# Attention and two MoE layers on one core: gates moved into ScalarE's copies of transposes, scalings over three engines, later weight decoding

## The chip, the cores and the metric

One core of one Trainium2 chip runs the whole program. Its engines work side by side, each through its own list of instructions in order: TensorE (PE; its weight loads are PEld), VectorE (DVE), ScalarE (ACT), GpSimd (POOL) and SyncE (SP, which issues DMAs). An instruction starts when the one ahead of it has gone and the semaphores that it waits for have come. The metric is the device time of the program in microseconds; less is better.

## The reference

Float32 throughout. `q`, `k`, `v` are (4, 8, 576, 64): batches, heads, positions, columns.

```
a     = softmax(causal(q k^T / 8));   local = a v
mem   = (phi(q) M_prev) / (phi(q) z_prev + 1e-6);   phi(x) = max(x,0) + exp(min(x,0))
g     = sigmoid(beta)                        # one number per head
x     = g * mem + (1 - g) * local            # then 2304 tokens x 512
h     = x w_in;   x = (h - tanh(h)) w_out    # MoE layer 1, 512 -> 2048 -> 512
h     = x w_in2;  out = (P(h) / Q(h)) w_out2 # MoE layer 2, rational gate
```

The MoE weights arrive as float64 words and are turned into float32 on the chip.

## The kernel before, in words

**Attention.** Two heads make a pair; there are 16 pairs (4 batches x 4). Queries come in four row blocks of 128 (`i` = 0 to 3) and one of 64 rows for both heads together (`i` = 4). For each block `scores` multiplies on PE, `least` (DVE) copies the masked scores out of PSUM and takes the row's extreme, `expo` (ACT) takes exp and the row's sum, `recip` (DVE) inverts the sum, `scale` multiplies the probabilities `p` by 1/sum and by (1 - g) (POOL, nine times per pair), `turn` (PE) transposes them into a PSUM tile `tp`, `turned` (ACT) copies that to the SBUF tile `pT`, and `values` (PE) multiplies by v. The memory part runs beside it: `phi1` to `phi3`, `norm1` to `norm3` (1/norm times g is multiplied into phi), `phiT` (PE transposes), `phiC` (ACT's copy to SBUF), `memory` (PE). Both parts add up in the PSUM tiles `pv` and `pw`; `leave` (DVE) copies these to `x`. A pair's last copies are `x<-pv` (512 columns) and `x<-pw` (64).

**Weights.** Each MoE layer has 16 chunks `f`, each with two pieces `s` (w_in, w_out). A piece is decoded by `w_decode`: ACT Abs (L575), then four DVE steps (L577, L578, L582, L585). `w_split` makes a high part (ACT, L595) and a low part (POOL, L597). `w_keep` writes the decoded piece to DRAM, and `w_back` fetches it later and splits it (ACT L618, DVE L621). `Background.tick` moves every piece in work on by one step and may start one more.

**MoE layer 1.** An item is one chunk on one tile of tokens. Four chunks (0 to 3) run on 9 tiles of 256 tokens (36 small items), the other 12 on 6 tiles of 384 (72 items). Each item has 12 matmuls in its head (`h`, L1049), the gate (ACT tanh L1078, DVE L1079, ACT high part `gh` L1084, DVE low part `gl` L1085), and 12 matmuls in its tail (`y`, L1096). The tokens' own split `xs` (L1040 ACT, L1041 POOL) is made once per tile. Layer 2 has 96 items of 384 tokens.

**What sets the order.** The attention stage is laid out by a table: event `name` of pair `n` has the time 100 n + `AT[name]`, or `OVER[n][name]` in place of it, and the events are written into the engines' lists in that order. `FILL` places small MoE heads (`h`), token splits (`xs`) and background steps (`bg`) in every period of 100, the steps only from `BG_FROM` on, and only some of them may start a new piece after `MIX_FROM`. The heads' gates and tails follow at fixed offsets. What is left of the 36 small items when the table ends is run by `advance` in a loop, one item and one `tick` per turn. Then come the 72 items with further ticks, then layer 2.

Of the kernel before, what the change touches and what calls it, by code (L numbers as in the profile page):

```python
# [19 lines left out]
P = 128  # L20
# [9 lines left out]
BG_FROM = 411.57  # L30
N_PT = 6
AGE_A, AGE_B, AGE_C = 1, 3, 4

AT = {'s1': 48.5,
 's2': -9.21,
 's3': 21.3,
 's4': 70.44,
 'm0': 4.97,
 'm1': 62.46,
 'm2': 5.74,  # L40
 'm3': 33.51,
 'm4': 78.23,
 'x00': 30.93,
 'x01': 24.67,
 'x10': 102.19,
 'x11': 85.19,
 'x20': 18.5,
 'x21': 19.67,
 'x30': 58.64,
 'x31': 69.14,  # L50
 'x40': 109.89,
 'r0': 37.01,
 'r1': 108.02,
 'r2': 41.21,
 'r3': 76.67,
 'r4': 118.34,
 'c00': 74.77,
 'c01': 56.83,
 'c10': 122.27,
 'c11': 119.0,  # L60
 'c20': 56.26,
 'c21': 59.04,
 'c30': 108.12,
 'c31': 89.73,
 'c40': 130.65,
 't0': 80.11,
 't1': 78.69,
 't2': 125.39,
 't3': 124.44,
 't4': 141.98,  # L70
 't5': 169.93,
 't6': 143.99,
 'k0': 102.22,
 'k1': 88.5,
 'k2': 137.01,
 'k3': 127.14,
 'k4': 158.58,
 'k5': 173.99,
 'k6': 164.4,
 'v0': 154.99,  # L80
 'v1': 165.34,
 'v2': 165.15,
 'v3': 157.91,
 'v4': 214.1,
 'mpv': 135.18,
 'mpw': 207.69,
 'opv': 193.7,
 'opw': 216.87,
 'f0': 96.55,
 'f1': 107.92,  # L90
 'g0': 111.95,
 'g1': 119.11,
 'phi1': -43.41,
 'phi2': -30.03,
 'phi3': -19.86,
 'norm1': 0.16,
 'norm2': 31.56,
 'norm3': 32.06,
 'load_k': 31.4,
 'load_q': -0.43,  # L100
 'load_n': 22.21,
 'load_v': 69.9}
OVER = {0: {'s1': -246.08,
     's2': -489.04,
     's3': -438.03,
     's4': -268.61,
     'm0': -364.53,
     'm1': -58.91,
     'm2': -376.8,
     'm3': -354.5,  # L110
     'm4': -107.2,
     'x00': -253.7,
     'x01': -333.4,
# [204 lines left out]
     'x10': 53.22,
     'x11': 53.59,
     'x20': 19.69,  # L320
     'x21': 35.75,
     'x30': 38.43,
     'x31': 65.04,
     'x40': 88.75,
     'r0': 40.06,
     'r1': 63.48,
     'r2': 52.17,
     'r3': 69.87,
     'r4': 94.42,
     'c00': 49.51,  # L330
     'c01': 71.71,
     'c10': 122.1,
     'c20': 58.79,
     'c30': 101.38,
     'c31': 107.83,
     'c40': 106.11,
     't0': 77.35,
     't1': 84.46,
     't2': 111.03,
     't3': 124.81,  # L340
     't4': 129.29,
     't5': 169.94,
     't6': 175.76,
     'k0': 79.21,
     'k1': 86.74,
     'k2': 118.15,
     'k3': 137.94,
     'k4': 146.79,
     'k5': 174.32,
     'k6': 181.98,  # L350
     'v0': 151.75,
     'v1': 164.52,
     'v2': 161.24,
     'v3': 147.01,
     'v4': 206.58,
     'mpv': 119.31,
     'mpw': 202.36,
     'opv': 179.54,
     'opw': 233.46,
     'f0': 100.8,  # L360
     'f1': 111.34,
     'g0': 105.32,
     'g1': 167.75,
     'phi1': -49.32,
     'phi2': -26.17,
     'phi3': -17.57,
     'norm1': -9.26,
     'norm2': 14.37,
     'norm3': 23.54,
     'load_k': 6.62,  # L370
     'load_q': 11.44,
     'load_n': 20.81,
     'load_v': 100.48},
 4: {'s1': 35.05,
     's2': -12.86,
     's3': -4.6,
     's4': 71.3,
     'm0': 1.53,
     'm1': 55.25,
     'm2': 12.98,  # L380
     'm3': 36.56,
     'm4': 82.1,
     'x00': 43.45,
     'x01': 2.11,
     'x10': 76.35,
     'x11': 85.28,
     'x21': 17.28,
     'x30': 60.58,
     'x31': 70.56,
     'x40': 103.3,  # L390
     'r0': 57.92,
     'r1': 88.17,
     'r2': 33.4,
     'r4': 122.54,
     'c00': 68.21,
     'c01': 59.63,
     'c10': 102.54,
     'c11': 117.17,
     'c20': 45.05,
     'c21': 56.72,  # L400
     'c30': 107.47,
     'c31': 91.4,
     'c40': 131.13,
     't0': 89.95,
     't2': 128.1,
     't3': 129.22,
     't4': 121.75,
     't5': 166.87,
# [41 lines left out]
KEEP = 5  # L450
# [1114 lines left out]
```

## Time and profile before

| | us |
|---|---|
| median of 3 runs | 1038.77 (1038.48 to 1040.22) |
| the profiled execution | 1039.35 |
| its span, first to last instruction | 1037.6 |
| PE busy | 1010.9 (97%) |
| DVE, ACT, POOL busy | 784.7, 701.5, 362.6 |

PE's busy time is modelled and is not PE at its peak, so the table alone doesn't say where time can be had. The stages of the span can be told by PE's lines: attention to 252.84 us (with small items in between), the rest of the small items to 328.41 us, the 72 items to about 633 us, layer 2 to the end.

### The profile page before, as it was taken

What the parts mean: (1) busy time and instruction counts of PE and PEld (TensorE: products, weight loads), DVE (VectorE), ACT (ScalarE), POOL (GpSimd) and SP (SyncE); (2) the same over time, 40 slices, a digit from 0 to 9 for tenths busy, and PEclk for the clock granted to TensorE, in tenths of its full rate; (3) what the DMA queues carried; (4) which work ended last, traced back from release to release, by engine and by line L of the source; (5) the groups of instructions that cost most, each with busy time, mean ns of one, the idle gap of its engine ahead of it and who ended that gap; (6) DMA issues with size and microseconds to landing.
All of it is one profiled execution on the core that took longest, in us unless ns stands there. A gap on an engine that the chain in (4) does not pass through costs nothing.

```text
span 1037.6 us, 18004 instructions
## 1 busy us (share of the span) xinstructions
PE 1010.9 (97%) x6446; PEld 912.2 (88%) x6446; DVE 784.7 (76%) x1759; ACT 701.5 (68%) x1492; POOL 362.6 (35%) x380
## 2 busy tenths in 40 slices
PE   7999999999988999999999999999999999999998
PEld 4766777888988999999999999999999999999997
DVE  5889999874878366757676767987877877877885
ACT  5878877785555443333333556998888888888886
POOL 4878896673543010101000101332332423323221
PEclk9999999999999999999999999999999999999999
DMA  4445556432232124444444441000000000000000
GB/s 131 124 148 146 166 133 203 140 109 73 82 103 82 41 92 122 122 128 128 136 126 123 141 144 41 21 1 32 1 11 22 1 31 1 1 31 1 22 10 31
DMA packets 37674, 82.97 MB, mean 80 GB/s; under 512 B 8528, under 2 KB 11088, under 8 KB 37584
## 3 DMA queue, kind: packets, MB, share of 16 engines
q1 hardware_dynamic: 37120, 81.55, 26.1%
q8 instruction: 51, 0.84, 0.3%
q14 instruction: 39, 0.32, 0.1%
q10 hardware_dynamic: 464, 0.27, 0.1%
HBM read 66.07 MB, written 15.73 MB: 79 GB/s over the span
## 4 chain that ended last, share of the span: by engine, by line
PE 80%; DVE 12%; ACT 4%; issue 2%; POOL 1%; DMA 0%; SPq 0%; DVEq 0%; ACTq 0%; POOLq 0%
PE h L1049 35%; PE y L1179 19%; PE y L1096 17%; PE s L857 3%; DVE p L873 3%; PE tp L925 2%; PE pv L974 2%; DVE wf L585 2%; DVE wf L582 1%; ACT p L886 1%; DVE gl L1085 1%; DVE wf L577 1%; DVE phi L789 1%; PE pw L974 1%; DVE wf L578 1%
## 5 line engine op out<-in xcount | busy, mean ns | idle before, releaser
L1049 PE MATMUL h<-xs,w 128*128 128x384 f32 (+1 forms) x2448 | 437.4, 327 | 1.6 <-POOL xs L1041 0.7
L1049 PEld LDWEIGHTS h<-xs,w 128*128 128x128 f32 x2448 | 408.2, 188 | 12.5 <-POOL xs L1041 1.3
L1096 PE MATMUL y<-gh,w 128*128 128x384 f32 (+1 forms) x864 | 216.3, 318 | 3.0 <-ACT gh L1084 2.9
L1179 PE MATMUL y<-w,gh 128*128 128x512 f32 x576 | 179.6, 393 | 0.0
L1096 PEld LDWEIGHTS y<-gh,w 128*128 128x128 f32 x864 | 152.2, 189 | 4.3 <-ACT gh L1084 3.1
L1096 PE MATMUL y<-gl,w 128*128 128x384 f32 (+1 forms) x432 | 137.6, 318 | 4.0 <-DVE gl L1085 3.9
L1041 POOL TENSOR_TENSOR xs<-x,xs 128x256 fp32r<-128x256 f32 (+1 forms) x56 | 51.3, 940 | 256.1 <-ACT xs L1040 232.8
L1078 ACT ACTIVATE g<-h 128x384 f32<-128x384 f32 (+1 forms) x108 | 49.2, 455 | 134.6 <-PE h L1049 121.0
L1079 DVE TENSOR_TENSOR g<-h,g 128x384 f32<-128x384 f32 (+1 forms) x108 | 55.2, 512 | 97.2 <-ACT g L1078 97.0
L906 POOL TENSOR_SCALAR p<-p,sm,omg 128x256 f32<-128x256 f32 (+4 forms) x143 | 109.2, 773 | 48.8 <-DVE sm L898 34.7
L1179 PEld LDWEIGHTS y<-w,gh 128*128 128x128 f32 x576 | 106.8, 188 | 17.4
L1179 PE MATMUL y<-w,gl 128*128 128x512 f32 x288 | 114.0, 396 | 0.2
L1168 POOL TENSOR_TENSOR gl<-g,gh 128x384 fp32r<-128x384 f32 x48 | 49.5, 1031 | 149.8 <-ACT gh L1166 149.8
L1168 POOL TENSOR_TENSOR gl<-vG,gh 128x384 fp32r<-128x384 f32 x47 | 50.3, 1070 | 131.2 <-ACT gh L1166 129.0
L886 ACT ACTIVATE p<-p,sm 128x128 f32<-128x128 f32 (+4 forms) x144 | 84.9, 592 | 12.2 <-DVE sm L873 8.3
L1084 ACT CAST gh<-g 128x384 fp32r<-128x384 f32 (+1 forms) x108 | 51.6, 478 | 61.2 <-PE y L1096 58.6
L1096 PEld LDWEIGHTS y<-gl,w 128*128 128x128 f32 x432 | 81.6, 189 | 5.2 <-DVE gl L1085 5.2
L1155 DVE TENSOR_TENSOR vA<-vA,vC 128x384 f32<-128x384 f32 x96 | 53.5, 558 | 42.9 <-ACT vC L1149 42.9
L873 DVE CUSTOM_DVE_ANT_0 p<-s,mask 128x512 f32<-128x512 f32 (+4 forms) x160 | 69.5, 478 | 17.3 <-PE s L857 15.2
L1085 DVE TENSOR_TENSOR gl<-g,gh 128x384 fp32r<-128x384 f32 (+1 forms) x108 | 61.8, 573 | 23.6 <-ACT gh L1084 23.6
L857 PE MATMUL s<-rk,rq 64*128 64x512 f32 (+5 forms) x320 | 71.9, 475 | 7.8 <-DVE sm L873 5.1
L1144 DVE SCALAR_TENSOR_TENSOR vA<-vA,vC 128x384 f32<-128x384 f32 x96 | 59.3, 618 | 25.2 <-ACT vC L1143 20.1
(95 smaller groups left out, 1607.2 us busy)
## 6 DMA issues: line engine op xcount, KB each, us to landing
wraw<-in_w_in_dram SPq DMA_DIRECT2D x32, 512.0 KB, 4.1
wraw<-in_w_out_dram SPq DMA_DIRECT2D x32, 512.0 KB, 4.0
wk<-wf SPq DMA_DIRECT2D x42, 256.0 KB, 4.4
wx<-wk SPq DMA_DIRECT2D x21, 512.0 KB, 3.3
qn<-in_qn_dram SPq DMA_DIRECT2D x16, 320.0 KB, 3.7
vn<-in_vn_dram SPq DMA_DIRECT2D x16, 320.0 KB, 4.3
out_dram<-o SPq DMA_DIRECT2D x18, 256.0 KB, 2.0
rk<-in_kd_dram SPq DMA_DIRECT2D x30, 144.0 KB, 2.8
```

Of the source, the lines that this page charges most:

```text
L857: nc.tensor.matmul(bank[:, c0:c0 + k1 - k0], d["rq"][r, q0:q0 + P], d["rk"][r, k0:k1], start=True, stop=True, skip_group_check=True,)
L873: nc.vector.tensor_tensor_reduce(out=v["p"][-1][:, k0:k1], in0=bank[:, c0:c0 + k1 - k0], in1=mask, scale=-0.125, scalar=3.0e38, op0=ALU.ad ...
L886: nc.scalar.activation(pt, pt, AF.Exp, bias=sm[:, 4 + e:5 + e], scale=-1.0, accum_out=sm[:, 2 * e:2 * e + 1],)
L906: eng.tensor_scalar(pt, pt, v["sm"][:, 6 + e:7 + e], og[:, c:c + 1], ALU.mult, ALU.mult)
L1049: nc.tensor.matmul(ps[:, 0:T], wi_of(layer, f, wp, k), xs[k][:, xp], start=(n == 0), stop=(n == 3 * NK - 1),)
L1079: nc.vector.tensor_tensor(v["g"], v["h"], v["g"], ALU.subtract)
L1085: self.lo.tensor_tensor(v["gl"], v["g"], v["gh"].bitcast(F32), ALU.subtract)
L1096: nc.tensor.matmul(ps, wo_of(1, f, w)[:, m * P:(m + 1) * P], v[g], start=(first and j == 0 and m % n == 0), stop=(last and j == 2), skip_g ...
L1144: nc.vector.scalar_tensor_tensor(A, A, QEPS, C, ALU.add, ALU.mult)
L1155: nc.vector.tensor_tensor(n["A"], n["A"], n["C"], ALU.mult)
L1168: eng.tensor_tensor(o["gl"], o["G"], o["gh"].bitcast(F32), ALU.subtract)
L1179: nc.tensor.matmul(acc_of[t][m], g[:, c], wo_of(2, f, w), start=(first and j == 0), stop=(last and j == 2),)
```

## The change

- `g` no longer goes into `norm2`. `phiC`'s ACT copy multiplies by it, with a column of scalars (`g4`) as its scale.
- For the row blocks 0, 2 and 3 (`LATE`), (1 - g) no longer goes into `scale`; it becomes the scale of ACT's copy in `turned`. Blocks 1 and 4 keep both factors in `scale`.
- The nine scalings of a pair are spread by `SCALES`: two on ACT (128x128 and 128x512), one on DVE (128x384), six on POOL.
- The last block's two extremes are put together with a reduce into another column.
- The low parts of layer 1's chunks that are decoded after attention go to DVE in place of POOL; those decoded in attention stay on POOL.
- `KEEP` falls from 5 to 1: one chunk, not five, is decoded in attention, written to DRAM and fetched back; eleven, not seven, are decoded directly after attention.
- A new table: background steps start later, six places per period in place of four, and the small heads start later. The program has 4 small heads and 1 tail ahead of the last matmul of attention, where it had 13 and 13.
- In the stage of 72 items steps come by a list (`TICKS_1`), and pieces of layer 2 start at least three ticks apart (`EVERY`).
- `banks`, `inside` and `N_P` are set so that nothing else changes: `PSUM_DECODE` is False, `N_P` is 1, `MIX` is True.

```diff
-BG_FROM = 411.57
+BG_FROM = 1157.58
+SCALES = "APPPPVAPP"
+LATE = (0, 2, 3)
+LOW_ATT, LOW_POST, LOW_X = "P", "V", "P"
 AT = {
- 's1': 48.5,
+ 's1': 85.61,
...
 FILL = {
- 'h': [-68.87, -232.13],
+ 'h': [-1954.49, 128.27],
- 'bg': [(-191.13, 0, 1), (187.94, 1, 1), (73.53, 0, 0), (51.79, 0, 0)],
+ 'bg': [(248.62, 1, 1), (198.68, 1, 1), (6.75, 1, 0), (59.81, 1, 0), (22.12, 1, 0),
+        (36.08, 1, 0)],
...
-KEEP = 5
+KEEP = 1
...
@@ Background.tick
+                and (self.q[self.ns][2][0] == 1 or self.now >= self.last + EVERY)
...
@@ norm2
             nc.vector.reciprocal(nrm, nrm)
-            gg = self.cp["g"][:, h:h + 2].unsqueeze(1)
-            nc.vector.tensor_tensor(nrm, nrm, gg.to_broadcast([P, NQ + 1, 2]), ALU.mult)
@@ phiC
-            nc.scalar.copy(d["phiT"][:, j0:j0 + w], d.pop(("php", k))[:, 0:w])
+            nc.scalar.activation(
+                d["phiT"][:, j0:j0 + w], d.pop(("php", k))[:, 0:w], AF.Copy,
+                scale=self.cp["g4"][:, n % NP:n % NP + 1],
+            )
@@ scale
-            eng = nc.vector if (n, i, e) == (0, NQ - 1, 0) else nc.gpsimd
-            eng.tensor_scalar(
-                pt, pt, v["sm"][:, 6 + e:7 + e], og[:, c:c + 1], ALU.mult, ALU.mult
-            )
+            how = "V" if (n, i, e) == (0, NQ - 1, 0) else SCALES[2 * i + e]
+            eng = nc.vector if how == "V" else nc.gpsimd
...
+            elif how == "A":
+                nc.scalar.activation(pt, pt, AF.Copy, scale=r)
+            else:
+                eng.tensor_scalar(pt, pt, r, None, ALU.mult)
@@ turned
-            nc.scalar.copy(t[:, 0:w, :].rearrange("r t c -> r (t c)"), ps[:, 0:w * P])
+            if i in LATE:
+                c = 2 * (n % NP) + e
+                nc.scalar.activation(
+                    dst, ps[:, 0:w * P], AF.Copy, scale=self.cp["omg"][:, c:c + 1]
+                )
+            else:
+                nc.scalar.copy(dst, ps[:, 0:w * P])
@@ after attention
-            bg.add(1, f, w_direct, slot_of[f], nc.gpsimd)
+            bg.add(1, f, w_direct, slot_of[f], ENG[LOW_POST])
@@ the 72 items
-            bg.tick()
-            if t > 0:
+            for _ in range(TICKS_1[s % nf] if t else 1):
                 bg.tick()
```

Three places show how the engines' lists move. The first is ACT in attention, one pair. In the kernel before, with `p` the probabilities, `tp` the transposes and `wf` a piece in decoding:

```order
L938 COPY pT_5_965<-tp_5_954 128x512
L886 ACTIVATE p_1_0_924,sm_99<-p_1_0_924,sm_99 128x256
L938 COPY pT_6_979<-tp_6_967 128x128
L886 ACTIVATE p_1_1_926,sm_99<-p_1_1_926,sm_99 128x256
L575 ACTIVATE wf_0_0_985<-wraw_0_0_918 128x512
L938 COPY pT_0_1011<-tp_0_989 128x512
L886 ACTIVATE p_113,sm_102<-p_113,sm_102 128x576
L829 COPY phiT_1001<-php_0_1002 128x512
L938 COPY pT_1_1039<-tp_1_972 128x512
```

And in the changed kernel, the same stretch of a middle pair:

```order
L966 COPY pT_5_1668<-tp_5_1663 128x512
L901 ACTIVATE p_1_1_1653,sm_100<-p_1_1_1653,sm_100 128x256
L799 ACTIVATE phi_1672<-phi_1672 128x640
L841 ACTIVATE phiT_1680<-php_0_1681,g_98 128x512
L927 ACTIVATE p_0_0_1579<-p_0_0_1579,sm_99 128x128
L901 ACTIVATE p_1_0_1651,sm_100<-p_1_0_1651,sm_100 128x256
L901 ACTIVATE p_114,sm_103<-p_114,sm_103 128x576
L927 ACTIVATE p_3_0_1629<-p_3_0_1629,sm_102 128x512
L962 ACTIVATE pT_0_1733<-tp_0_1716,omg 128x512
L962 ACTIVATE pT_1_1751<-tp_1_1721,omg 128x512
```

Two scalings (L927) have come in, the copies (L841, L962) carry a factor, and no decoding stands here any more.

The second place is DVE between attention and the 72 items, where `g` and `gl` are the gates of the small items and `w` the low part of a weight piece. Before:

```order
L577 TENSOR_SCALAR wf_8_0_4340<-wf_8_0_4340 128x512
L578 TENSOR_SCALAR wf_8_0_4340<-wf_8_0_4340 128x512
L1079 TENSOR_TENSOR g_7_1_4384<-h_7_1_4363,g_7_1_4384 128x256
L1085 TENSOR_TENSOR gl_7_0_4388<-g_7_0_4344,gh_7_0_4387 128x256
L582 SCALAR_TENSOR_TENSOR wf_8_0_4340<-wraw_8_0_4213,wf_8_0_4340 128x512
L585 SCALAR_TENSOR_TENSOR wf_8_0_4340<-wraw_8_0_4213,wf_8_0_4340 128x512
L1079 TENSOR_TENSOR g_7_2_4424<-h_7_2_4403,g_7_2_4424 128x256
L1085 TENSOR_TENSOR gl_7_1_4428<-g_7_1_4384,gh_7_1_4427 128x256
```

After:

```order
L608 TENSOR_TENSOR w_8_4046<-wf_8_1_4048,w_8_4046 128x512
L590 SCALAR_TENSOR_TENSOR wf_9_1_4139<-wraw_9_1_4011,wf_9_1_4139 128x512
L594 SCALAR_TENSOR_TENSOR wf_9_1_4139<-wraw_9_1_4011,wf_9_1_4139 128x512
L1107 TENSOR_TENSOR g_6_2_4223<-h_6_2_4201,g_6_2_4223 128x256
L1113 TENSOR_TENSOR gl_6_1_4227<-g_6_1_4182,gh_6_1_4226 128x256
L608 TENSOR_TENSOR w_9_4215<-wf_9_0_4101,w_9_4215 128x512
L1107 TENSOR_TENSOR g_6_3_4273<-h_6_3_4244,g_6_3_4273 128x256
L1113 TENSOR_TENSOR gl_6_2_4277<-g_6_2_4223,gh_6_2_4276 128x256
L608 TENSOR_TENSOR w_9_4215<-wf_9_1_4139,w_9_4215 128x512
L585 TENSOR_SCALAR wf_10_0_4271<-wf_10_0_4271 128x512
L586 TENSOR_SCALAR wf_10_0_4271<-wf_10_0_4271 128x512
```

A fifth instruction per piece (L608) now stands between the gates.

The third place is ACT at the last small items (tile 8), just ahead of the 72 items. Before:

```order
L1078 ACTIVATE g_8_2_4587<-h_8_2_4567 128x256
L1084 CAST gh_8_1_4590<-g_8_1_4548 128x256
L595 CAST w_9_4622<-wf_9_0_4510 128x512
L575 ACTIVATE wf_9_1_4624<-wraw_9_1_4420 128x512
L595 CAST w_9_4622<-wf_9_1_4624 128x512
L575 ACTIVATE wf_10_0_4639<-wraw_10_0_4583 128x512
L1078 ACTIVATE g_8_3_4641<-h_8_3_4608 128x256
```

After:

```order
L1106 ACTIVATE g_8_2_4556<-h_8_2_4535 128x256
L1112 CAST gh_8_1_4559<-g_8_1_4516 128x256
L606 CAST w_11_4475<-wf_11_1_4477 128x512
L606 CAST w_12_4596<-wf_12_0_4514 128x512
L583 ACTIVATE wf_12_1_4603<-wraw_12_1_4552 128x512
L1106 ACTIVATE g_8_3_4605<-h_8_3_4577 128x256
L1112 CAST gh_8_2_4608<-g_8_2_4556 128x256
```

Before, ACT's Abs and high part of one piece (`wf_9_1`) stood in front of the last gate, with DVE's four steps between the two; now two high parts stand there, of which the second waits for DVE's last two steps.

## Rows read from the trace of the kernel before

**Rows 1.** The page's first part, PE: busy us, share, instructions.

```profile
PE 1010.9 (97%) x6446; PEld 912.2 (88%) x6446; DVE 784.7 (76%) x1759; ACT 701.5 (68%) x1492; POOL 362.6 (35%) x380
```

**Rows 2.** Windows: stretch, length, busy us (instructions) by engine, clock, DMA.

```profile
31.20:65.30 34.10, 32.95 (x328) 23.74 (x327) 26.08 (x109) 28.03 (x80) 26.37 (x34) 1.00 0.51 158
65.30:212.10 146.80, 139.99 (x1270) 109.08 (x1269) 133.06 (x434) 114.40 (x317) 116.50 (x122) 0.99 0.53 155
...
252.84:328.41 75.57, 67.88 (x545) 65.29 (x541) 57.37 (x103) 43.48 (x106) 32.84 (x32) 0.99 0.25 77
328.41:633.20 304.79, 304.53 (x1754) 303.79 (x1754) 197.21 (x338) 124.19 (x245) 29.01 (x26) 1.00 0.40 118
```

**Rows 3.** Timeline of DVE: pairs' copies to x; start us, length us.

```profile
31.23 0.67 DVE L1233 COPY x<-pv 128x512 f32<-128x512 f32 x1
...
65.29 0.67 DVE L1233 COPY x<-pv 128x512 f32<-128x512 f32 x1
...
242.45 0.68 DVE L1233 COPY x<-pv 128x512 f32<-128x512 f32 x1
...
250.06 0.69 DVE L1233 COPY x<-pv 128x512 f32<-128x512 f32 x1 [2.35 <-PE pv L974]
```

**Rows 4.** Timeline of PE: heads of small items, then the first of 72.

```profile
252.84 4.46 PE L1049 MATMUL h<-xs,w 128*128 128x256 f32 x36
...
306.83 1.56 PE L1049 MATMUL h<-xs,w 128*128 128x256 f32 x12
...
309.63 1.68 PE L1049 MATMUL h<-xs,w 128*128 128x256 f32 x12
...
328.41 2.88 PE L1049 MATMUL h<-xs,w 128*128 128x384 f32 x12
```

**Rows 5.** Groups over the whole span: ACT copies and gates, POOL scalings, ACT high parts.

```profile
L906 POOL TENSOR_SCALAR p<-p,sm,omg 128x256 f32<-128x256 f32 (+4 forms) x143 | 109.2, 773 | 48.8 <-DVE sm L898 34.7
L938 ACT COPY pT<-tp 128x512 f32<-128x512 f32 x96 | 55.3, 584 | 19.4 <-PE tp L925 19.2
L938 ACT COPY pT<-tp 128x128 f32<-128x128 f32 x16 | 4.1, 259 | 1.7 <-PE tp L925 1.7
L1148 ACT ACTIVATE vA<-h 128x384 f32<-128x384 f32 x96 | 46.9, 489 | 39.4 <-PE h L1049 37.4
L1152 ACT ACTIVATE g<-h,coef 128x384 f32<-128x384 f32 x48 | 31.5, 656 | 0.0
L595 ACT CAST w<-wf 128x512 fp32r<-128x512 f32 x22 | 13.6, 617 | 11.2 <-DVE wf L585 11.2
L621 DVE TENSOR_TENSOR w<-wx,w 128x512 fp32r<-128x512 f32 x42 | 30.0, 758 | 2.9 <-PE h L1049 1.8 <-ACT w L618 1.2
```

**Rows 6.** Timeline of DVE, small items after attention.

```profile
303.83 0.42 DVE L577 TENSOR_SCALAR wf<-wf 128x512 f32<-128x512 f32 x1
...
304.63 0.42 DVE L1079 TENSOR_TENSOR g<-h,g 128x256 f32<-128x256 f32 x1
...
305.29 0.69 DVE L582 SCALAR_TENSOR_TENSOR wf<-wraw,wf 128x512 uint32<-128x512 uint32 x1
...
306.63 0.42 DVE L1079 TENSOR_TENSOR g<-h,g 128x256 f32<-128x256 f32 x1
...
310.96 1.51 DVE L577 TENSOR_SCALAR wf<-wf 128x512 f32<-128x512 f32 x1
...
313.83 0.41 DVE L1079 TENSOR_TENSOR g<-h,g 128x256 f32<-128x256 f32 x1
```

**Rows 7.** Timeline of POOL, beside the last two rows of the group above.

```profile
310.72 2.91 POOL L597 TENSOR_TENSOR w<-wf,w 128x512 fp32r<-128x512 f32 x2
```

**Rows 8.** Groups by line, 252.84 to 328.41: token splits.

```profile
L1041 POOL TENSOR_TENSOR xs<-x,xs 128x256 fp32r<-128x256 f32 x20 | 15.6, 810 | 34.5 <-ACT xs L1040 34.5
```

**Rows 9.** What PE waited for, 252.8 to 330: us in total, times, longest.

```profile
PE y L1096 <- DVE gl L1085: 3.9, 5, 1.5
PE y L1096 <- ACT gh L1084: 2.9, 1, 2.9
```

More of the change, by code (lines that the diff above doesn't have):

```diff
@@ new lines @@
+AT = {'s1': 85.61,
+ 's2': 26.67,
+ 's3': 53.17,
+ 's4': 110.31,
+ 'm0': 44.4,
+ 'm1': 90.48,
+ 'm2': 37.92,
+ 'm3': 82.89,
+ 'm4': 117.78,
+ 'x00': 65.98,
+ 'x01': 79.86,
+ 'x10': 125.15,
+ 'x11': 114.36,
+ 'x20': 72.88,
+ 'x21': 52.13,
+ 'x30': 99.9,
+ 'x31': 100.57,
+ 'x40': 129.75,
+ 'r0': 87.48,
+ 'r1': 130.64,
+ 'r2': 83.82,
+ 'r3': 107.62,
+ 'r4': 161.65,
+ 'c00': 123.36,
+ 'c01': 121.41,
+ 'c10': 142.14,
+ 'c11': 149.12,
+ 'c20': 100.65,
+ 'c21': 87.47,
+ 'c30': 132.7,
+ 'c31': 123.9,
+ 'c40': 185.26,
+ 't0': 127.28,
+ 't1': 129.28,
+ 't2': 153.1,
+ 't3': 144.31,
+ 't4': 157.88,
+ 't5': 206.11,
+ 't6': 198.66,
+ 'k0': 132.91,
+ 'k1': 140.52,
+ 'k2': 166.01,
+ 'k3': 157.51,
+ 'k4': 185.9,
+ 'k5': 206.14,
+ 'k6': 205.84,
+ 'v0': 216.43,
+ 'v1': 220.08,
+ 'v2': 187.34,
+ 'v3': 214.03,
+ 'v4': 234.49,
+ 'mpv': 176.77,
+ 'mpw': 234.57,
+ 'opv': 232.79,
+ 'opw': 256.45,
+ 'f0': 112.99,
+ 'f1': 179.31,
+ 'g0': 119.5,
+ 'g1': 191.99,
+ 'phi1': 7.32,
+ 'phi2': 19.47,
+ 'phi3': 29.5,
+ 'norm1': 32.06,
+ 'norm2': 53.37,
+ 'norm3': 64.56,
+ 'load_k': 79.77,
+ 'load_q': 62.89,
+ 'load_n': 80.12,
+ 'load_v': 106.17}
@@ L447 @@
+EXTRA = {'setup2': -331.29, 'load_m0': -278.12, 'load_n1': -235.41}
+FILL = {'h': [-1954.49, 128.27],
+ 'xs': [-204.12, -672.01, -1149.02, -309.47, 924.98],
+ 'bg': [(248.62, 1, 1), (198.68, 1, 1), (6.75, 1, 0), (59.81, 1, 0), (22.12, 1, 0),
+        (36.08, 1, 0)],
+ 'gate1': 79.13,
+ 'gate2': 265.61,
+ 'tail': 320.17,
+ 'leave': 384.43,
+ 'end': 8175.82}
 WARM = {0: 2, 2: 2}
 LESS_AT = 4
-KEEP = 5
+KEEP = 1
 LAG = 4
@@ L672, in tick @@
                 _, done, key, work, _ = self.q[self.ns]
+                self.last = self.now
                 self.ns += 1
@@ L1328 @@
     for f in FA:
[L1329 removed]
+        bg.add(1, f, w_direct, f"wa{f}", ENG[LOW_ATT])
     for f in FB[len(FB) - KEEP:]:
@@ L1357 @@
         at, _, name, n = heapq.heappop(events)
-        if attn.done and not mixed:
+        if MIX and attn.done and not mixed:
             mixed = True
@@ L1411 @@
             bg.less()
+        if left <= 2:
+            bg.banks = None
         if left == 0 and two is None:
```

794 lines of the change are left out of this document (367 added, 427 removed).

## The prediction, made before the changed kernel ran

> **What bounds the kernel now.** I read the page's busy times first [rows 1]: PE is busy 97% of the span, but its time is modelled, so the stages have to be told apart. The windows do that [rows 2]. From 328.41 us on PE is busy 304.53 of 304.79 us and runs at its pace; nothing that the change does there can take time away, only add. Before that there are two stages with room. In attention the first pairs carry neither decoding nor MoE items: three of them take 65.29 - 31.23 = 34.1 us, 11.35 each [rows 3], with PE busy 32.95 of 34.10, ACT 28.03 and DVE 26.08 [rows 2]. From 65.30 to 212.10 decoding and items are mixed in, and nine pairs take 146.8 us, 16.3 each; there DVE is busy 133.06 us, 91%, the highest share of DVE in any stretch [rows 2]. So bare attention is paced by PE, and attention with decoding by DVE. From 252.84 to 328.41 PE runs the rest of the small items. One item takes 309.63 - 306.83 = 2.80 us where nothing stalls, so a half (12 matmuls) takes 1.40 [rows 4]. By the order of PE's list this stretch holds 23 heads and 22 tails, 45 halves, 63.0 us; it took 75.6, so 12.6 us are lost. The waits name 3.9 us of it as tails waiting for DVE's low part of a gate, and 2.9 us as one wait for ACT's high part [rows 9], just ahead of the 72 items.
>
> The sum is therefore three terms: when attention ends, how many small halves are left then, and what is lost while they run.
>
> **Attention, pairs 0 to 9.** The profiled pair 0 ends at 31.23 us [rows 3]; the new table does the same work in it, and I leave it (1.5 us either way). Pairs 1 to 9 now carry no decoding and no items. PE's work in a pair is unchanged. POOL loses three of nine scalings of 0.77 us [rows 5], 2.3 us a pair, of 26.37 / 3 = 8.8 [rows 2]; it had room already. DVE gains one scaling of 384 columns and loses two small operations: its 26.08 / 3 = 8.7 us go to about 9.0. ACT gains most. A column of scalars as scale or bias is priced by two ACT operations from the same PSUM tile, 656 ns with two such columns and 489 with none [rows 5], so 84 ns each; six copies per pair get one, 0.50 us. The scaling of 128x128 is not in the trace; the copy of that size takes 259 ns, so 0.34 with its column (0.26 to 0.43). That of 128x512 lies between the PSUM copy of that size, 584, and the SBUF cast with two columns, 617 + 168; I take 617 + 84 = 0.70, since its source is SBUF [rows 5]. Together 1.5 us, which makes ACT 9.3 + 1.5 = 10.9 us a pair, beside PE's 11.35. A pair can thus not be under 11.35. If ACT can be filled only to the 82% that it has in the bare pairs now, a pair takes 10.9 / 0.82 = 13.3. I take the 91% at which DVE set the pace: 10.9 / 0.91 = 12.0, and 9 x 12.0 = 108.0.
>
> **Pairs 10 to 15.** By the new order pair 10 decodes one piece and pairs 11 to 13 two each; pairs 12 to 14 hold one head each. A piece's four DVE steps cost 0.80 + 1.34 = 2.1 us where POOL stays away (from 303.83 to 304.63, and from 305.29 to 306.63) [rows 6]. Two pieces and a gate make DVE's 9.0 into 13.6, at 91% 14.9 us; before, such pairs took 16.3 with about an item each. One piece: 13.0. Pair 14, almost bare: 12.0. The last pair takes 250.06 - 242.45 = 7.6 [rows 3], as before, since no scores of a next pair are in it, and the last matmuls of `pw` end 2.8 us after its copy starts. Sum: 31.2 + 108.0 + 13.0 + 3 x 14.9 + 12.0 + 7.6 + 2.8 = 219.3, against 252.8: **-33.5 us**. With 11.35 and 13.3 in place of 12.0 it is -39 and -22.
>
> **Small items moved behind attention.** Before, 13 heads and 13 tails ran in attention, now 4 and 1. Up to the first head of the 72 there are 66 halves in place of 45: 21 x 1.40 = **+29.4 us**. So nearly all of the gain is paid back on PE, which had these items half for nothing, beside a DVE that could not follow.
>
> **What is lost while they run.** The decoding goes with them: about two pieces per three items, each with its low part now on DVE too. On DVE three items' gates take 3 x 0.66 (304.63 to 305.29) = 2.0, two pieces 4.3, and two low parts 2 x 0.68 (758 ns in the same form [rows 5], less the 0.08 by which neighbours overlap) = 1.4: 7.6 us against PE's 8.4. What eats the room is POOL: beside a low part on POOL [rows 7] two DVE steps that take 0.80 took 313.83 - 310.96 = 2.87 [rows 6]. The low parts leave POOL, its token splits stay, 4 x 0.81 = 3.2 us per tile of four items [rows 8]. If DVE loses half of that, 0.4 us per item, it needs 2.9 per item to PE's 2.8: just over. I keep the loss seen today, 3.9 us over six tiles, as 0.65 for each of eight, 5.2. The wait of 2.9 us goes: the last gate's high part stood behind a piece whose four DVE steps had still to run, and now it waits for two of them, 1.3 us, while PE has a tail and a head (2.8 us) to do. Of the remaining 5.8 us of today (the slow stretches around these waits) I keep half. Loss 8.1 in place of 12.6: **-4.5 us**. The bounds are 4 us (only the first waits) and 23 (DVE blocked, below).
>
> **At no cost.** The 72 items: DVE is busy 197.21 of 304.79 us and ACT 124.19 [rows 2], which covers the five pieces that now run over into them; without that cover, at most 2 us. The steps by list and the spacing of starts act only there. Fewer pieces go to DRAM and back, so SP's queue gets shorter, and the DMA engines were at most 53% busy. No wait is added on PE.
>
> Sum: -33.5 + 29.4 - 4.5 = -8.6 us. From the profiled execution's 1039.35 that gives 1030.8; it lay 0.6 above the median of the runs, so **1030 us**, with 1025 to 1036 as this case's own range.
>
> **Rivals.**
>
> *PE sets the pace everywhere.* ACT, with 10.9 of 11.35 us, keeps up: for it speaks that all three engines stood over 75% in the bare pairs without slowing PE; against it, that every engine works strictly in order. 9 x 0.65 = 5.9 us less, and the loss falls to 5: 1021.
>
> *ACT becomes the bound in attention.* At 13.1 us per pair: 9 x 1.1 = 10 us more, 1040, no change. For it: 1.5 us on the engine that was second busiest there [rows 2]. Against: the copies with a factor are the old copies, and two scalings no longer wait for POOL.
>
> *DVE paces the small items, and the kernel gets slower.* The place is 220 to 315 us. It decides once three items' work on DVE, with what POOL's splits hold up, passes PE's 8.4 us. With low parts at the full 0.76 it is 7.8; if DVE stands still for all of POOL's 0.81 per item it is 10.2, 0.6 per item over. Over the 29 items with decoding that is 17 us, in place of 5.2: 1042. For it: 2.87 in place of 0.80. Against it: beside that same POOL work DVE did get two steps done, and in the changed kernel POOL is idle three quarters of the time. The Trainium skill ("SBUF — State Buffer", section "Who interferes with whom") says that the port pair which DVE and GpSimd share is locked for a whole instruction and that the loser fully blocks, which is this rival's mechanism; that the stretched steps here came to an end while POOL went on [rows 6, 7] fits a lock that changes hands at each instruction, nearer to half than to all.
>
> *Nothing comes of it.* The gates and scalings are only redistributed, and the moved items cancel the shorter attention: 1038.
>
> **How the numbers follow.** This kernel's measurements can tell 0.2% from no change, some 2.1 us: 1036.7 to 1040.8. Forecast 0.54; PE everywhere 0.12; ACT bound 0.12; DVE paces 0.15; nothing 0.07. Faster: 0.54 + 0.12 and 0.02 of the ACT case, 0.68. Same: the nothing case and 0.06 of the ACT case, with 0.01 of the DVE case, 0.14. Slower: the rest, 0.18. The range leaves out what is better than PE everywhere and the worst of the DVE case, where both bounds meet: 1020 to 1044.
>
> **What the profile will show.** Copies `x<-pv` 11.4 to 12.5 us apart in pairs 2 to 9 with ACT over 88% busy; 13.3 there means ACT bounds. The last `pw` matmul at 214 to 225 us. Heads of small items 2.8 to 3.0 us apart; over 3.2, with tails waiting for DVE's `gl`, DVE paces. No wait of about 3 us ahead of the first 128x384 head. The same 304 to 306 us from there to layer 2. The forecast is wrong if attention ends after 230 us, or if the small items lose over 14 us.

## The result, and the profile after

| | before | after |
|---|---|---|
| median, us | 1039.35 (1038.48 to 1040.22, 4 runs) | 1026.11 (1025.57 to 1026.36, 4 runs) |
| the profiled execution, its span | 1039.35, 1037.6 | 1025.57, 1023.8 |

The ratio is 0.9872, 95% interval 0.9855 to 0.9889: faster by 13.2 us, where 8.6 to 8.8 were forecast.

The page's first part answers to [rows 1]; each entry is an engine's busy us, share of the span and instructions.

```profile
PE 1008.8 (99%) x6446; PEld 905.9 (88%) x6446; DVE 770.4 (75%) x1775; ACT 722.7 (71%) x1523; POOL 324.2 (32%) x319
```

POOL has lost 38 us and ACT gained 21; PE's busy time hardly moved. As before, the stages tell where the time went. The windows of the changed kernel, in the columns of [rows 2]: four pairs without decoding, three pairs with two pieces each, the end of attention to the first 384-token head, the 72 items.

```profile
90.96:138.88 47.92, 47.92 (x458) 33.58 (x456) 35.95 (x154) 45.32 (x121) 33.70 (x33) 1.00 0.47 141
...
151.79:193.56 41.77, 41.24 (x379) 30.63 (x378) 40.53 (x142) 40.90 (x106) 35.35 (x31) 1.00 0.61 174
...
216.60:315.38 98.78, 96.23 (x794) 93.58 (x794) 78.36 (x159) 61.83 (x151) 26.80 (x32) 1.00 0.34 105
315.38:619.00 303.62, 303.18 (x1754) 302.98 (x1753) 196.21 (x348) 123.04 (x244) 25.12 (x24) 1.00 0.39 117
```

The copies that end each pair, from DVE's timeline (start us, length us), answer to [rows 3]:

```profile
102.94 0.67 DVE L1261 COPY x<-pv 128x512 f32<-128x512 f32 x1
...
114.92 0.67 DVE L1261 COPY x<-pv 128x512 f32<-128x512 f32 x1
...
126.90 0.67 DVE L1261 COPY x<-pv 128x512 f32<-128x512 f32 x1
...
138.88 0.67 DVE L1261 COPY x<-pv 128x512 f32<-128x512 f32 x1
```

They stand 11.98 us apart, to the hundredth, and the first window names PE: it is busy for all of 47.92 us. The chain of work that ended last, followed back from 115 to 102.6 us, stands on PE alone. From 151.79 to 193.56 it stands on DVE. First the one, then the largest shares of the other:

```profile
by line: PE s L872 34.8%; PE tp L946 25.7%; PE pv L1002 20.9%; PE pv L986 6.9%; PE pw L1002 5.9%; PE php L834 4.4%; PE pw L986 2.9%
```

```profile
by line: DVE p L888 27.5%; DVE wf L594 11.0%; DVE wf L590 9.6%; DVE wf L586 7.9%; DVE x L1261 6.2%; issue 5.7%; DVE wf L585 5.5%; DVE nrm L818 5.4%; DVE phi L803 5.3%; DVE sm L913 3.6%; DVE p L929 3.0%; DVE phi L795 2.9%; DVE sm L910 2.7%; 
```

DVE is busy for 40.53 of 41.77 us there and waits for no other engine. PE (41.24) is close behind it: three pairs at 11.98 and one head of the small items in each, at 1.40, would by themselves take it 40.1 us.

PE's timeline of small heads, then the first of 384 tokens, answers to [rows 4]:

```profile
220.74 4.36 PE L1077 MATMUL h<-xs,w 128*128 128x256 f32 x36
...
310.19 1.56 PE L1077 MATMUL h<-xs,w 128*128 128x256 f32 x12
315.38 2.26 PE L1077 MATMUL h<-xs,w 128*128 128x384 f32 x12
```

And what PE waited for there (us in total, times, longest), which answers to [rows 9]:

```profile
PE h L1077 <- POOL xs L1069: 1.8, 6, 0.5
PE h L1077 <- ACT y L1142: 0.4, 1, 0.4
PE y L1124 <- ACT gh L1112: 0.3, 1, 0.3
PE y L1124 <- ACT y L1142: 0.2, 1, 0.2
```

No tail waits for DVE's low part of a gate any more, and the one wait of 2.9 us for ACT's high part is down to 0.3. For the token splits `xs` PE waited before the change too, but less; this line belongs to [rows 9]:

```profile
PE h L1049 <- POOL xs L1041: 0.7, 3, 0.3
```

The account of the span: attention ends at 216.60 in place of 252.84 (-36.2); 21 more halves of small items run behind it (+29.4); 98.78 us for 66 halves of 1.40 loses 6.4 in place of 12.6 (-6.2); from the first 384-token head to the end there are 708.4 us in place of 709.2 (-0.8). Together -13.8, from 1037.6 to 1023.8.

### The profile page after: what moved, and what is told of

It is laid out like the page before. It is cut to its first block, busy times and chain, and to the rows that moved or that the text cites. A ratio compares the mean times of both kernels' runs of the same rounds, so it can differ in the third digit from the quotient of the medians.

```text
span 1023.8 us, 17988 instructions
## 1 busy us (share of the span) xinstructions
PE 1008.8 (99%) x6446; PEld 905.9 (88%) x6446; DVE 770.4 (75%) x1775; ACT 722.7 (71%) x1523; POOL 324.2 (32%) x319
## 4 chain that ended last, share of the span: by engine, by line
PE 85%; DVE 8%; ACT 2%; POOL 2%; issue 1%; DMA 1%; ACTq 0%; SPq 0%; DVEq 0%; POOLq 0%
PE h L1077 36%; PE y L1207 19%; PE y L1124 18%; PE s L872 4%; PE tp L946 3%; PE pv L1002 2%; DVE p L888 2%; POOL xs L1069 1%; DVE wf L594 1%; PE pv L986 1%; DVE wf L590 1%; PE pw L1002 1%; ACT p L901 1%; DVE wf L586 0%; PE php L834 0%
## 5 line engine op out<-in xcount | busy, mean ns | idle before, releaser
L1124 PE MATMUL y<-gh,w 128*128 128x384 f32 (+1 forms) x864 | 214.0, 316 | 0.6 <-ACT gh L1112 0.3
L901 ACT ACTIVATE p<-p,sm 128x128 f32<-128x128 f32 (+3 forms) x144 | 83.6, 586 | 6.0 <-DVE sm L888 6.0
L1113 DVE TENSOR_TENSOR gl<-g,gh 128x384 fp32r<-128x384 f32 (+1 forms) x108 | 58.4, 541 | 29.6 <-ACT gh L1112 29.5
L1176 ACT ACTIVATE vA<-h 128x384 f32<-128x384 f32 x96 | 46.9, 489 | 39.4 <-PE h L1077 37.4
L872 PE MATMUL s<-rk,rq 64*128 64x384 f32 (+5 forms) x320 | 70.3, 471 | 2.0 <-DMA rq<-in_qd_dram 1.6
```

The costliest lines, as they stand in the source:

```text
L872: nc.tensor.matmul(bank[:, c0:c0 + k1 - k0], d["rq"][r, q0:q0 + P], d["rk"][r, k0:k1], start=True, stop=True, skip_group_check=True,)
L901: nc.scalar.activation(pt, pt, AF.Exp, bias=sm[:, c:c + 1], scale=-1.0, accum_out=sm[:, 2 * e:2 * e + 1],)
L1113: self.lo.tensor_tensor(v["gl"], v["g"], v["gh"].bitcast(F32), ALU.subtract)
L1124: nc.tensor.matmul(ps, wo_of(1, f, w)[:, m * P:(m + 1) * P], v[g], start=(first and j == 0 and m % n == 0), stop=(last and j == 2), skip_g ...
```

## Experiments

Each kernel is compared with the kernel before by a ratio with its 95% interval, since several chips were used; "after" is the changed kernel (0.9872). Of times within 2 us of each other the times alone don't settle the order.

### What moving the low parts to DVE is worth

**The changed kernel with its direct low parts on POOL** (1033.09 us; 0.9947, 0.9935 to 0.9960), and **the kernel before with them on DVE** (1033.65 us; 0.9954, 0.9940 to 0.9967):

```
-LOW_ATT, LOW_POST, LOW_X = "P", "V", "P"      # changed kernel
+LOW_ATT, LOW_POST, LOW_X = "P", "P", "P"
-            bg.add(1, f, w_direct, slot_of[f], nc.gpsimd)   # kernel before
+            bg.add(1, f, w_direct, slot_of[f], nc.vector)
```

> The changed kernel with the low parts of the pieces decoded after attention back on POOL; nothing else differs. Theory A (port contention beside the gates cost the time): the small items after attention, which now take 98.8 us and lose 6.3, lose about 6 us more, as in the kernel before, with tails waiting for DVE's gl again by 3 to 5 us; 1030 to 1034. Theory B (the loss fell only because the last gates no longer stand behind a whole piece on ACT): no change beyond 1 us, 1026. Attention itself ends at the same 216.6 us in both.

> The kernel before with only this part of the change: the low parts of the pieces decoded after attention on DVE. Theory A: the wait of tails for gl (3.9 us) shrinks to under 1 and the loss of 12.6 us to about 8, so 1034 to 1036 against 1039. Theory B: the wait of 2.9 us ahead of the 72 items and the slow stretch around it stay, so at most 1 us less: 1038. Rival: DVE gets overfilled and the loss grows: over 1040.

What PE waited for from 215 to 335 us, in the changed kernel with low parts on POOL:

```profile
PE y L1124 <- DVE gl L1113: 4.5, 6, 1.5
PE h L1077 <- POOL xs L1069: 1.4, 5, 0.5
PE y L1124 <- ACT gh L1112: 1.2, 1, 1.2
```

The waits for `gl` are back as they were before the change. In the kernel before with the low parts on DVE none of them is left, and only the single wait for `gh` is (2.6 us of 2.9), so the two waits have different causes.

The medians differ by 7.0 us in the changed kernel and by 4.8 us in the kernel before. Of the 7.0 us, 5.8 stand in the stage of the small items (104.5 us in place of 98.7); 1.2 lie ahead of the first copy to `x` (30.71 us in place of 29.54), where the edit does nothing. In the kernel before the stage takes 70.7 us in place of 75.5, the whole difference.

With the low parts DVE has 17 more instructions in that stage, but hardly more work, since its other steps get shorter: 78.36 us for 159 instructions, where it had 77.21 for 142. The first line is that stage with the low parts on POOL, to be read against the third window of the changed kernel above; then come DVE's `gl` there and in the changed kernel:

```profile
217.80:322.28 104.48, 97.17 (x793) 93.92 (x792) 77.21 (x142) 61.87 (x151) 49.40 (x49) 1.00 0.33 99
```

```profile
L1113 DVE TENSOR_TENSOR gl<-g,gh 128x256 fp32r<-128x256 f32 x33 | 20.2, 613 | 0.9 <-ACT gh L1112 0.9
```

```profile
L1113 DVE TENSOR_TENSOR gl<-g,gh 128x256 fp32r<-128x256 f32 x33 | 15.3, 464 | 0.9 <-ACT gh L1112 0.9
```

**The token splits on DVE too** (1027.02 us; 0.9885, 0.9870 to 0.9900):

```
-LOW_ATT, LOW_POST, LOW_X = "P", "V", "P"
+LOW_ATT, LOW_POST, LOW_X = "P", "V", "V"
```

> The changed kernel with the token splits of the small items after attention on DVE, so that POOL does nothing there. Theory A (two engines at one port cost the time): no contention is left, the splits take DVE 4 x 0.33 per tile, PE no longer waits 0.25 per tile for them, and the loss of 6.3 us falls by 1 to 3: 1023 to 1025. Theory B (DVE has no room: 7.6 us per three items and 1.0 for the splits against PE's 8.4): PE waits for gl and the loss grows, 1028 or more.

PE's waits there, from 200 to 340 us:

```profile
PE y L1124 <- DVE gl L1113: 2.9, 4, 0.8
```

The 1.8 us for `xs` are gone, and 2.9 us for `gl` have come. With POOL out of that stage DVE's own steps are shorter (a low part 684 ns for 779, `gl` 419 for 464), but 10.3 us of splits came with it. Nothing is won by the last piece of POOL's work.

### What sets the pace of a pair

**No gate factors** (the gates are left out of the six ACT copies of a pair, and so of the computation; 1025.33 us; 0.9874, 0.9861 to 0.9888):

```
-                nc.scalar.activation(
-                    dst, ps[:, 0:w * P], AF.Copy, scale=self.cp["omg"][:, c:c + 1]
-                )
+                nc.scalar.copy(dst, ps[:, 0:w * P])
```

> The changed kernel with plain copies in place of the six copies per pair that multiply by a gate; the gates g and (1 - g) of blocks 0, 2, 3 and of the memory part are left out of what is computed. It prices the columns of scalars: 687 against 584 ns. Theory A (ACT sets the pair): ACT gets 0.6 us lighter and a pair 0.4 to 0.6 us shorter, 4 to 7 us in all: 1019 to 1022. Theory B (PE sets the pair, its list has no gap in 102 to 127 us): 11.98 stays and the time with it, 1026.

Two pairs of it, in the windows' columns:

```profile
89.68:113.64 23.96, 23.96 (x230) 16.79 (x230) 17.97 (x78) 21.86 (x61) 16.84 (x17) 1.00 0.40 114
```

ACT has 10.9 us a pair in place of 11.3, and the pair is 11.98 again: ACT is filled to 95% without setting the pace.

**The old gates and scalings in the new table** (the gate in `norm2`, both factors in `scale`, all nine scalings on POOL; 1039.28 us; 1.0000, 0.9992 to 1.0009):

```
-SCALES = "APPPPVAPP"
-LATE = (0, 2, 3)
+SCALES = "PPPPPPPPP"
+LATE = ()
...
+            nc.vector.tensor_tensor(nrm, nrm, gg.to_broadcast([P, NQ + 1, 2]), ALU.mult)
```

> The changed kernel, its table and its decoding, with the gates and scalings of the kernel before: g in norm2, (1 - g) in all nine scalings, all on POOL with two scalars, plain copies. It tells what the gates and the spreading bring by themselves. Theory A (PE sets the bare pairs, and the shorter attention comes from moving decoding and items out): the pairs stay within 0.5 us of 11.98, and the time within 1026 to 1032. Theory B (POOL's scalings are what held the pairs): pairs of 13 us or more, 1040 or more.

Its windows: four pairs without decoding, then three with it.

```profile
98.86:146.78 47.92, 47.92 (x458) 33.59 (x460) 35.75 (x153) 40.13 (x113) 34.43 (x45) 1.00 0.48 143
...
159.84:207.46 47.62, 43.86 (x381) 31.54 (x381) 46.38 (x141) 38.47 (x100) 38.12 (x40) 1.00 0.54 152
```

The whole gain is lost, but not in the bare pairs: those take the same 47.92 us with the same 458 matmuls. It is lost in the first pairs (the copies at 33.34 and 98.86 in place of 29.54 and 90.96) and in the pairs with decoding, 47.62 us in place of 41.77. There DVE has 141 instructions in place of 142, but 46.38 us of work in place of 40.53. The groups say which grew. DVE, the three pairs with decoding (busy us, mean ns of one), first with the old gates, then in the changed kernel:

```profile
L888 DVE CUSTOM_DVE_ANT_0 p<-s,mask 128x512 f32<-128x512 f32 x9 | 6.0, 689 | 0.0
L594 DVE SCALAR_TENSOR_TENSOR wf<-wraw,wf 128x512 uint32<-128x512 uint32 x6 | 5.5, 918 | 0.2
L585 DVE TENSOR_SCALAR wf<-wf 128x512 f32<-128x512 f32 x6 | 4.1, 689 | 0.0
L822 DVE TENSOR_TENSOR nrm<-nrm,gg 128x10 f32<-128x10 f32 x3 | 2.1, 686 | 0.1
```

```profile
L888 DVE CUSTOM_DVE_ANT_0 p<-s,mask 128x512 f32<-128x512 f32 x9 | 5.9, 683 | 0.0
L594 DVE SCALAR_TENSOR_TENSOR wf<-wraw,wf 128x512 uint32<-128x512 uint32 x6 | 4.6, 766 | 0.2
L585 DVE TENSOR_SCALAR wf<-wf 128x512 f32<-128x512 f32 x6 | 2.7, 453 | 0.0
```

The copy of scores, whose input `s` is in PSUM, has nearly the same length in both; the two decoding steps shown, from SBUF to SBUF, are 20% and 52% longer, and a product of 10 columns, 0.17 us in the bare pairs, takes 0.69 us on average. The Trainium skill ("SBUF — State Buffer", section "Who interferes with whom") has it so: a DVE instruction contends with a GpSimd instruction that reads SBUF if both its own inputs lie in SBUF, and with GpSimd in a mode that uses the shared port pair; with one SBUF input outside those modes it does not. The trace fits both kinds, though no run shows in which mode a step with one SBUF input, such as L585, ran. The size does not follow from how long POOL is busy, though: here that is 80% of the window, in 40 instructions, and in the changed kernel it is 85%, in 31.

This run also prices the table. It and the kernel before with the low parts on DVE have the old gates and the same engine for the low parts, and differ by the rest of the change, the table above all: 1.0000 against 0.9954. So with the old gates the new table loses about 5 us, and it pays only together with the new ones. What the new gates and scalings would bring in the old table no run shows.

**ACT's two scalings on DVE** (1038.58 us; 0.9998, 0.9989 to 1.0007):

```
-SCALES = "APPPPVAPP"
+SCALES = "VPPPPVVPP"
```

> The changed kernel with the two ACT scalings of a pair on DVE (three there now). DVE has 9.0 busy us of 11.98 in a bare pair and 97% in the decoding pairs. Theory A (PE sets the bare pairs, DVE the decoding pairs): 11.98 stays, pairs 11 to 13 grow by up to 0.8 us each, 1026 to 1029. Theory B (ACT is still what limits somewhere): less than 1025.

One of these scalings, in the timelines of DVE and of POOL:

```profile
104.45 1.71 DVE L929 TENSOR_SCALAR p<-p,sm 128x512 f32<-128x512 f32 x1
```

```profile
104.34 1.55 POOL L809 TENSOR_TENSOR pz<-phi,z 128x640 f32<-128x640 f32 x1 [1.21 <-DVE sm L910]
```

DVE's scaling starts 0.11 us after POOL's instruction and ends 0.27 us after that one ends at 105.89; the one of 384 columns, at 111.57, took 0.42, and a decoding step of 512 columns in this kernel (L585, mean of six) 0.41. So one instruction of POOL can hold DVE for its whole length, and the table, laid out for ACT, sets the two side by side in every pair. Bare pairs take 12.3 us, those with decoding 16.4. All the gain is gone.

**All nine scalings on POOL** (after's gates; 1059.45 us; 1.0204, 1.0190 to 1.0218):

```
-SCALES = "APPPPVAPP"
+SCALES = "PPPPPPPPP"
```

> The changed kernel with all nine scalings of a pair on POOL (six of them by one scalar, as now three). Theory A (ACT, 11.3 of 11.98 us busy, is what keeps a pair over PE's own 11.4): ACT gets 1.1 us lighter and pairs 5 to 9 take 11.4 to 11.7, so 2 to 5 us less: 1022 to 1024. Theory B (POOL is the one that can't take more: a one-scalar scaling of 512 columns takes it 1.57 us in the trace, so nine make it 8.4 + 3.7 = 12.1 us or more of a pair): pairs take 13 or more, 1040 or more.

Four pairs of it without decoding (6 to 9), from copy to copy:

```profile
113.26:164.20 50.94, 48.79 (x458) 33.50 (x460) 34.36 (x150) 42.76 (x113) 48.60 (x45) 1.00 0.45 138
```

POOL is busy 95% of it, and the copies stand 12.73 us apart, a little under the 13 of theory B. That is 3 us of the 33 lost. The copy of pair 5 comes 22.3 us late (113.26 in place of 90.96): up to 97 us PE's transposes waited 13.6 us for POOL's one-scalar scalings. Pairs 10 to 13 lose another 8. But the old gates had all nine on POOL too, and kept 11.98. The difference is the form: the scaling with one scalar (128x512, 40 to 139 us of the changed kernel) takes 1572 ns, and the one with two, which does a multiplication more, took 775 in the old gates' kernel. That asked for the next two.

**A column of ones as second scalar** (the same result; 1024.36 us, 1023.14 to 1026.47; 0.9859, 0.9846 to 0.9873), and **the same with all nine on POOL** (1034.20 us; 0.9960, 0.9948 to 0.9973):

```
-                eng.tensor_scalar(pt, pt, r, None, ALU.mult)
+                eng.tensor_scalar(pt, pt, r, self.cp["one"], ALU.mult, ALU.mult)
...
+SCALES = "PPPPPPPPP"      # the second of the two only
```

> The changed kernel with a second scalar, a column of ones, in the three scalings per pair on POOL (and the one on DVE) that have one scalar now; the result is the same. In the trace POOL takes 1572 ns for 512 columns with one scalar and took 918 with two before. Theory A (the form costs, not what runs beside it): POOL's group falls to about 900 and 830 ns. Theory B (DVE beside it costs): 1.3 to 1.5 us stay. For the time: PE sets a pair, so at most 2 us less from the first pairs and the decoding pairs, 1024 to 1026.

> The changed kernel with the column of ones, and all nine scalings of a pair on POOL: the run with one engine for the scalings (1059 us) again, but with the form of instruction that takes 0.85 in place of 1.57 us. Theory A (that run was slow by its form of instruction): pairs without decoding at 11.98 us again, POOL no longer waited for there, and not over 1032 us. Within it, if POOL's work holds up DVE's decoding steps, the three pairs with decoding go to 15.0 to 15.7 us (the kernel with the old gates had 15.6 to 16.4, with 0.7 us of gate multiplication on DVE in each), which gives 1028 to 1030 us; if not, 14 us and 1025 us. Theory B (one engine can't carry nine scalings in any form): 13 us or more in every pair, 1045 us or more.

POOL's groups from 40 to 139 us, first of the changed kernel, then with the ones:

```profile
L929 POOL TENSOR_SCALAR p<-p,sm 128x512 f32<-128x512 f32 x9 | 14.1, 1572 | 2.6 <-ACT p L901 2.3 <-DVE sm L913 0.3
```

```profile
L929 POOL TENSOR_SCALAR p<-p,sm,one 128x512 f32<-128x512 f32 x9 | 7.7, 852 | 8.6 <-DVE sm L913 6.4 <-ACT p L901 2.3
```

1572 ns become 852, and attention ends 2.1 us earlier (the last copy at 214.61 in place of 216.69), all of it gained by the copy of pair 5 (88.65 in place of 90.96), where transposes had waited for POOL's scalings. It is the fastest kernel measured. The 1.7 us by which its median is under the changed kernel's are as many as the trace shows, but the intervals of the two ratios overlap.

With all nine on POOL in that form the bare pairs are back at 11.98 us, so the 1059 us were the form's. The pairs with decoding take 14.4, 15.5 and 15.2, DVE's L585 693 ns. That is the hold-up again, at about the size expected; the time is 4 us over the 1028 to 1030 that it should have given. The first pairs took more than that: the copy of pair 5 is at 96.63, in place of 88.65, and up to 97 us transposes waited 5.6 us for POOL's scalings, in place of 1.5.

**DVE's scaling on POOL as well** (two scalars; 1026.78 us; 0.9881, 0.9868 to 0.9895):

```
-SCALES = "APPPPVAPP"
+SCALES = "APPPPPAPP"
```

> The changed kernel with a column of ones as second scalar in the one-scalar scalings, and the one scaling of a pair that stood on DVE (128x384, 0.42 us) given to POOL, so that POOL does seven of the nine. Theory A (the three pairs with decoding go at DVE's pace, 13.99 to 14.1 us with DVE busy in 97%, and what leaves DVE shortens them): 13.6 to 13.7 us each, attention ends 1 to 1.5 us earlier than with the column of ones alone, about 1023 us. Theory B (what POOL takes over it gives back by holding up DVE's decoding steps, which took 0.69 to 0.92 us in place of 0.45 to 0.77 where POOL did all nine scalings): 14.2 us or more each, 1025 us or more. Other pairs stay at 11.98 us by both.

The three pairs with decoding:

```profile
153.12:195.44 42.32, 41.64 (x380) 31.03 (x380) 40.88 (x138) 41.11 (x107) 32.62 (x34) 1.00 0.59 171
```

DVE has four instructions fewer than with the ones alone (142, 40.91 us), and as much to do: L590 went from 770 to 901 ns, L594 from 754 to 821. What left DVE it paid back beside POOL; 14.1 us a pair is neither the gain that theory A wanted nor quite the 14.2 of theory B, whose mechanism it has. The 2.4 us by which the run is slower than the one with the ones alone do not stand in these pairs: its copy of pair 5 is 3.7 us later (92.36 in place of 88.65).

### Where the decoding stands

**The old start and number of chunks decoded in attention, in the new table** (1065.02 us; 1.0250, 1.0236 to 1.0264):

```
-BG_FROM = 1157.58
+BG_FROM = 411.57
-KEEP = 1
+KEEP = 5
```

> The changed kernel with the decoding's old bounds: five expert tables' decoding begun in attention in place of the later start, so that some eight more pieces of four DVE steps (2.5 us a piece) stand in attention and that many fewer beside the small items. Theory A (a pair with two pieces goes at DVE's pace of 14 us and one without at PE's 11.98, so each four pieces cost 4 us): attention ends 6 to 9 us later; small items lose up to 2 us less; 1030 to 1034 us. Theory B (attention goes at PE's pace and hides decoding; only scalings and gates made the gain): attention ends within 1 us of the changed kernel's, 1024 to 1027 us.

DVE's copies from the start of the pairs where most of the pieces fell, and the window over these four pairs:

```profile
54.21 0.69 DVE L1261 COPY x<-pv 128x512 f32<-128x512 f32 x1 [0.83 <-PE pv L1002]
75.38 0.68 DVE L1261 COPY x<-pv 128x512 f32<-128x512 f32 x1
102.74 0.67 DVE L1261 COPY x<-pv 128x512 f32<-128x512 f32 x1
127.84 0.67 DVE L1261 COPY x<-pv 128x512 f32<-128x512 f32 x1
```

```profile
54.21:143.94 89.73, 64.95 (x503) 46.28 (x504) 81.17 (x217) 62.99 (x157) 51.54 (x45) 0.87 0.52 163
```

Both theories missed. Attention held 18 pieces in place of 10, the eight more that were expected, but the six places per period took 15 of them in four pairs, which went to 21.2, 27.4, 25.1 and 16.1 us, and PE stood still for 28% of that time, with a granted clock of 0.87 where it was 1.00 in the changed kernel. More than DVE's 2.5 us for each of the eight was lost. Two of PE's waits from 30 to 200 us, for the copies to `x` and for a DMA of queries:

```profile
PE pv L986 <- DVE x L1261: 8.0, 3, 3.7
PE s L872 <- DMA rq<-in_qd_dram: 7.8, 1, 7.8
```

Small heads then also started earlier (12 in attention in place of 4), so attention ended 58 us later and the stage behind it was 19 us shorter. So decoding in attention is dear, and dearest in a bunch; the run doesn't separate it from the items that follow it.

## Why the prediction was right, and where it wasn't

**Attention, pairs 1 to 9: the number was right, the reason was not.** I set 12.0 us by ACT, 10.9 us at 91%. The copies of pairs 6 to 9 stand 11.98 apart, and PE sets that: it is busy for the whole window, and neither taking ACT's factors away nor restoring the old gates moves it. That a share of 91%, taken over from DVE, came out at PE's pace is luck. The mean over the nine is 12.15, the first ones lengthened in part by POOL's one-scalar scalings (11.91 with the ones); the copies of pairs 2 to 4 stand 12.7 to 13.2 apart, outside the 11.4 to 12.5 that the profile was to show. The rival that PE sets the pace everywhere had this mechanism right, and its price wrong. "A pair can thus not be under 11.35" was a misreading of [rows 2, 3]. A pair has 458 / 4 = 114.5 matmul records, and the window of 34.1 us had 328, the work of 2.86 pairs, not of three; 34.1 / 2.86 = 11.9. Copies can stand three pairs apart with less than that between them, since the table may let part of a pair's work fall outside. (A few records may be missing from a trace; the 47.92 us of four pairs with the old gates do not hang on the count.) PE's pace per matmul was nearly the same before, 34.1 / 328 = 104 ns, as after, 47.92 / 458 = 105; by PE's busy time alone, 32.95 us, it was 100 before.

**ACT's prices** held: groups of ACT from 40 to 139 us of the changed kernel.

```profile
L962 ACT ACTIVATE pT<-tp,omg 128x512 f32<-128x512 f32 x32 | 20.9, 687 | 2.5 <-PE tp L946 1.9
L966 ACT COPY pT<-tp 128x512 f32<-128x512 f32 x16 | 9.3, 582 | 1.0 <-PE tp L946 1.0
L927 ACT ACTIVATE p<-p,sm 128x512 f32<-128x512 f32 x8 | 5.7, 718 | 0.0
L927 ACT ACTIVATE p<-p,sm 128x128 f32<-128x128 f32 x9 | 3.6, 398 | 0.0
```

A column as scale costs 687 - 582 = 105 ns (84 estimated). The Trainium skill ("ScalarE: Activation LUTs", section "What ACT_TABLE_LOAD costs") gives about 93 for each such operand, and the trace is somewhat above it. The scalings take 718 and 398 (700 and 340). ACT's pair is 45.32 / 4 = 11.3 us for 10.9. The rival that ACT becomes the bound had its load right and still fell, for at 95% ACT held nothing up: 0.4 us less of it per pair left the pair at 11.98.

**Pairs 10 to 15.** Pair 10 took 12.9 (13.0 predicted), pairs 11 to 13 13.9 each (14.9): there DVE sets the pace, as forecast, but it does not stop at 91%, it reaches 97%. Pair 10 is a hit by luck: DVE is busy for 86% of it, PE for all of it, and its 124 matmul records are 13.0 us at PE's 105 ns. Pair 14 took 11.5 (12.0), the last 9.0 (7.6). The first pair ended 1.7 us earlier than before, in part by chance, since two runs with the same attention have it at 29.85 and 30.71 us for 29.54. The end is 216.6 for 219.3.

**Moved items.** The count of 66 halves was the list's, so +29.4 holds by construction; what they took beyond 1.40 each is the next term.

**The loss among the small items: mis-sized, 6.4 for 8.1.** The term that failed is the 5.2 us of waits for `gl`; there were none. I had POOL's token splits take half of their time from DVE. With the low parts gone POOL is busy 27% of that stage, and what it holds up DVE makes good. In their place PE waits for `xs` itself, which I had not counted: 1.8 us by the waits, and six heads that open a tile of tokens took 1.62 to 3.09 us in place of 1.40, 4.6 us over together. The rival that DVE paces the small items had the mechanism (putting the low parts back brings the waits and 5.8 us in this stage) and the wrong trigger: it decides by how much POOL does, and the change took POOL's work away faster than it gave DVE any.

**At no cost** held: 303.62 us for the 72 items, for 304.79.

So the 13.8 us of the span, for 8.6 predicted, are 2.7 more in attention, 1.7 more among the small items, and 0.8 behind them.

**What the gates and the spreading are for** the prediction did not see; it had them as ACT's burden. In steps from the old gates in the new table: 1039.28; with the gates in ACT's copies 1034.20 (all on POOL, two scalars); spread over three engines 1024.36; in the form that the change uses, 1026.11. Both steps pay in the first pairs, where PE waits less for POOL's scalings, and in those with decoding, where DVE's steps are shorter; none pays through the bare pairs.

## What to carry to other kernels

Before a stretch's length is taken as an engine's pace, divide the instructions in it by those of one unit of work; markers that a schedule can shift do not bound whole units. Where DVE and POOL both work from SBUF, price a move between them by the rows of their neighbours too: giving DVE 17 low parts of POOL's made DVE's other steps shorter here (77.21 us for 142 instructions, then 78.36 for 159), and giving POOL a scaling of DVE's paid back what it saved. And after such a move look for the form of each instruction, not only its engine.

## What the runs showed of the hardware that was not expected

POOL's scaling by one column is slower than by two: 1572 against 852 ns for 128x512, and 1350 against 769 for 384 columns in the same stretch. A single DVE scaling that met a POOL instruction took 1.71 us and ended 0.27 us after it. The cause of the first is not known; no run looks inside it. With all nine scalings on POOL, the slower form left DVE's steps shorter: in the three pairs with decoding DVE took 41.04 us for 139 instructions, where POOL was busy 98% of the time, and 43.37 us for 138 beside the faster form, where POOL was busy 85%. Whether that is the form or only which instructions meet was not separated.
